# Turns for VectorE's two-operand work and GpSimd's work in the plan of an attention, expert layer and gated experts kernel

## The chip, the cores and the metric

The program runs on one core of a Trainium2 chip. The core has five engines that run side by side, each through its own queue of instructions in a fixed order, and that wait for each other through semaphores: TensorE (PE: matrix products; PEld is its loading of weights), VectorE (DVE), ScalarE (ACT), GpSimd (POOL) and SyncE (SP), which here only issues transfers. TensorE writes its results to PSUM; the working data of all engines lie in SBUF. The metric is the time of one execution on the device in microseconds (us); 1 ns is a thousandth of that.

## The reference

Three layers follow each other, all in float32; 4 x 576 = 2304 tokens, 512 wide.

```python
# band attention: 8 heads of 64, each query sees itself and the 127 before it
scores = scale * np.matmul(q, k.transpose(0, 1, 3, 2))
scores = np.where(mask, scores + bias[None], -1000000000.0)
attn = np.exp(scores - np.max(scores, axis=-1, keepdims=True))
attn = attn / (np.sum(attn, axis=-1, keepdims=True) + 1e-09)
x = np.matmul(attn, v)                     # then heads side by side: 2304 x 512
# first layer, 512 -> 2048 -> 512
h = np.maximum(x @ w_in, 0.0)
x = h * h @ w_out
# eight experts, 512 -> 1024 -> 512, weighted by a gate
P = np.exp(x @ w_gate - (x @ w_gate).max())
for _ in range(8):
    P /= P.sum(1, keepdims=True) + 1e-09
    P /= P.sum(0, keepdims=True) + 1e-09
    P *= N / E
for e in range(E):
    out += P[:, e:e + 1] * (np.maximum(x @ w1[e], 0.0) @ w2[e])
```

## The kernel before

**Numbers as pairs.** Each operand of a large product is split into a float16 part and a float16 remainder ("hi" and "lo"), and three of the four partial products are added. So each tile that feeds TensorE is made in two steps: ScalarE rounds it to hi (`g_hi`, `h_hi`, `ex_hi`, `t_hi`, ...), and then VectorE or GpSimd subtracts hi from the original and writes lo (`g_lo`, `ex_lo`, `t_lo` on VectorE; `h_lo`, `e_lo`, `w_lo` through the helper `minus` on GpSimd). Such a subtraction reads two operands from SBUF.

**The experts.** They take the last 1400 us or so. The eight experts of 1024 hidden columns are worked off in 16 groups `g` of 512 (half an expert), each for five blocks `j` of tokens (four blocks of 512 tokens and one, `j` = 1, of 256), in two parts `p`. Each block product is done as a 2 x 2 product with seven multiplications in place of eight, which costs sums of weights and of results. For a part the functions are:

- `g_prod` (L1427, TensorE): the seven products x @ w1, into the banks X, Y and Z of PSUM, six matrix products each of 256 columns (128 for the narrow block). `g_copy` (L1455, ScalarE) copies a bank to SBUF; `g_add` (L1459, VectorE) adds a bank of PSUM to such a copy ("a" from Z, "b" from Y, "c" from X); `g_relu` (L1467, ScalarE).
- `g_sum` (L1476 and, through `minus`, L396, GpSimd): four sums of the results, S1, S3, S2, S4, one after the other, each with two operands from SBUF. `g_hi` (L1486, ScalarE) and `g_lo` (L1490, VectorE) make the seven pairs `hp` for the second product.
- `o_prod` (L1509, TensorE): the seven products with w2, into banks oX, oY, oZ. `o_add` (L1535, VectorE) adds a bank, times the gate, to the output sums `acc_wc`, `acc_wd` and `x1`; two instructions in a wide block.
- the weights of a later group, while this one runs: `ex_load` (SyncE), `ex_sumsq` and `ex_scale` (a scale from the sum of squares), `ex_hi` (L1325, ScalarE) and `ex_lo` (L1329, VectorE) of the weights themselves, `ex_sums` (L1339 and L396 on `stage`, GpSimd: four sums), then `ex_hi` and `ex_lo` of these sums, 1024 columns in one instruction. `gates` (L1644, VectorE) makes the gate of the group.

**What sets the order.** The whole kernel is first written as some 11,000 units with an engine, a cost, a rank, the units that they wait for, and the buffers that they take and free (`unit` and `chain`, the class `Plan`). `Plan.run` then plays the program through with these costs: whenever an engine is free, it takes, of the units that are ready and whose buffers are free, the one with the lowest rank. The order in which units were taken is the order in which their instructions are written, engine by engine. On the chip only that order and the semaphores remain. Most units of the experts have the same lowest rank (`GEMM`) on VectorE, ScalarE and GpSimd, so the one that became ready first is taken; weight steps have a higher rank and come when nothing else is ready. The costs say, for 256 columns, 0.34 us on VectorE and 0.61 (0.69 for a `g_sum`) on GpSimd:

```python
    def c_dve(n, rate=1.04):
        return 0.07 + n * rate * 1e-3

    def c_pool(n):
        return 0.12 + n * 1.93e-3
```

## Time and profile before

| | |
|---|---|
| median of 3 runs | 2012.65 us (2009.2 to 2021.81) |
| the profiled execution, its own time | 2018.5 us |
| its span, first to last instruction | 2016.6 us |
| busy: TensorE | 1919.4 us (95%) |
| busy: VectorE | 1625.6 us (81%) |
| busy: ScalarE | 1259.6 us (62%) |
| busy: GpSimd | 982.9 us (49%) |
| TensorE's granted clock, mean | 0.99 of full |

The busy share of an engine is a mean over stages that differ, and ends of matrix products are modelled. A wait is told as engine, line and what released it. Lines are those of the kernel before; in the kernel after, lines behind the changed places stand 11 further on (L1490 is L1501, L1459 is L1470, L1535 is L1546, L1329 is L1340).

### The profile page before, as it was taken

What the parts mean: (1) busy time and instruction counts of PE and PEld (TensorE: products, weight loads), DVE (VectorE), ACT (ScalarE), POOL (GpSimd) and SP (SyncE); (2) the same over time, 40 slices, a digit from 0 to 9 for tenths busy, and PEclk for the clock granted to TensorE, in tenths of its full rate; (3) what the DMA queues carried; (4) which work ended last, traced back from release to release, by engine and by line L of the source; (5) the groups of instructions that cost most, each with busy time, mean ns of one, the idle gap of its engine ahead of it and who ended that gap; (6) DMA issues with size and microseconds to landing.
All of it is one profiled execution on the core that took longest, in us unless ns stands there. A gap on an engine that the chain in (4) does not pass through costs nothing.

```text
span 2016.6 us, 47090 instructions
## 1 busy us (share of the span) xinstructions
PE 1919.4 (95%) x18458; PEld 1689.7 (84%) x18458; DVE 1625.6 (81%) x3897; ACT 1259.6 (62%) x3434; POOL 982.9 (49%) x1198
## 2 busy tenths in 40 slices
PE   9799999999998899999999999999999999999999
PEld 9677888787886788888888888888888888888888
DVE  7797576464339988998989989898998989899887
ACT  6667576453346776766666666666666666666654
POOL 3444254357527554454545455454554545545432
PEclk9899999999999999999999999999999999999999
DMA  9343364220010010000101001000100101010002
GB/s 241 94 147 75 72 120 78 38 64 1 1 43 12 32 33 19 25 25 20 43 12 33 22 22 37 18 33 12 33 22 23 43 12 33 12 33 12 1 22 74
DMA packets 159662, 85.35 MB, mean 42 GB/s; under 512 B 112080, under 2 KB 144848, under 8 KB 159440
## 3 DMA queue, kind: packets, MB, share of 16 engines
q1 hardware_dynamic: 159440, 82.35, 15.7%
q8 instruction: 144, 2.36, 0.5%
q14 instruction: 78, 0.64, 0.1%
HBM read 64.50 MB, written 4.72 MB: 34 GB/s over the span
## 4 chain that ended last, share of the span: by engine, by line
PE 44%; DVE 33%; POOL 7%; ACT 6%; issue 6%; DMA 3%; SPq 0%; POOLq 0%; DVEq 0%; ACTq 0%
DVE hp L1490 10%; PE X L1427 9%; PE oX L1509 7%; PE h L1021 6%; PE y L1058 6%; DVE late L1329 6%; PE Y L1427 4%; PE oY L1509 3%; DMA stage<-in_moe_w_dram 2%; DVE acc_wc L1535 2%; DVE acc_wd L1535 2%; POOL stage L396 2%; DVE late L1459 2%; PE Z L1427 2%; ACT late L1325 2%
## 5 line engine op out<-in xcount | busy, mean ns | idle before, releaser
L1427 PEld LDWEIGHTS <-late 128*128 128x128 f16 x6720 | 617.7, 98 | 135.3 <-issue 67.8
L1509 PEld LDWEIGHTS <-hp 128*128 128x128 f16 x6048 | 585.8, 98 | 74.8 <-issue 9.9
L1509 PE MATMUL oX<-late,hp 128*128 128x256 f16 x3456 | 467.8, 273 | 5.9 <-DVE acc_wd L1535 4.1
L1490 DVE TENSOR_TENSOR hp<-late,hp 128x256 f16<-128x256 f32 (+1 forms) x662 | 317.8, 498 | 23.7 <-ACT hp L1486 19.7
L1486 ACT ACTIVATE hp<-late 128x256 f16<-128x256 f32 (+1 forms) x662 | 245.5, 388 | 72.4 <-POOL late L396 63.9
L1490 DVE TENSOR_TENSOR hp<-x,hp 128x256 f16<-128x256 f32 (+1 forms) x458 | 239.2, 531 | 25.6 <-ACT hp L1486 20.0
L1427 PE MATMUL Y<-y,late 128*128 128x256 f16 (+1 forms) x1920 | 241.3, 262 | 7.6 <-ACT late L1455 2.5
L1427 PE MATMUL X<-late 128*128 128x256 f16 (+1 forms) x1728 | 204.8, 254 | 35.3 <-DVE x L1459 16.8
L1509 PE MATMUL oY<-late,hp 128*128 128x256 f16 x1728 | 237.2, 273 | 0.0
L1021 PE MATMUL h<-xT,w_in 128*128 128x256 f16 x1728 | 221.0, 277 | 8.0 <-ACT r L1030 6.5
L1058 PE MATMUL y<-sq,w_out 128*128 128x256 f16 x1728 | 218.0, 274 | 0.9 <-DVE y L1126 0.9
L396 POOL TENSOR_TENSOR sq<-r,sq 128x256 f16<-128x256 f32 x144 | 108.5, 755 | 216.0 <-ACT sq L1044 210.2
L396 POOL TENSOR_TENSOR stage<-stage 128x256 f32<-128x256 f32 x210 | 178.9, 852 | 67.6 <-DVE late L1329 57.1
L1486 ACT ACTIVATE hp<-x 128x256 f16<-128x256 f32 (+1 forms) x458 | 174.1, 389 | 37.1 <-POOL x L396 27.3
L1467 ACT ACTIVATE late<-late 128x256 f32<-128x256 f32 (+1 forms) x295 | 114.8, 392 | 130.9 <-DVE late L1459 130.3
L1021 PEld LDWEIGHTS <-w_in 128*128 128x128 f16 x1728 | 169.1, 100 | 31.9 <-issue 8.6
L1058 PEld LDWEIGHTS <-w_out 128*128 128x128 f16 x1728 | 166.4, 99 | 23.8 <-issue 1.3
L396 POOL TENSOR_TENSOR late<-late 128x256 f32<-128x256 f32 (+1 forms) x211 | 170.0, 807 | 27.5 <-DVE hp L1490 15.3
L1329 DVE SCALAR_TENSOR_TENSOR late<-stage,es,late 128x512 f16<-128x512 f32 (+1 forms) x180 | 173.3, 988 | 4.5 <-ACT late L1325 2.9
L1325 ACT ACTIVATE late<-stage,es 128x512 f16<-128x512 f32 (+1 forms) x180 | 135.1, 783 | 43.0 <-POOL stage L396 37.4
L1427 PE MATMUL X<-form,late 128*128 128x256 f16 x1152 | 157.8, 273 | 3.4 <-DVE late L1459 2.6
L1036 DVE SCALAR_TENSOR_TENSOR r<-r,unit_s 128x256 f32<-128x256 f32 x112 | 68.5, 613 | 108.8 <-ACT r L1030 108.2
(230 smaller groups left out, 3093.1 us busy)
## 6 DMA issues: line engine op xcount, KB each, us to landing
stage<-in_moe_w_dram SPq DMA_DIRECT2D x60, 256.0 KB, 3.2
stage<-in_moe_w_dram SPq DMA_DIRECT2D x30, 512.0 KB, 3.7
st_in<-in_moe_w_in_dram SPq DMA_DIRECT2D x16, 512.0 KB, 6.5
st_out<-in_moe_w_out_dram SPq DMA_DIRECT2D x16, 512.0 KB, 5.5
raw_q<-in_q_dram SPq DMA_DIRECT2D x16, 256.0 KB, 4.7
raw_k<-in_k_dram SPq DMA_DIRECT2D x16, 256.0 KB, 4.5
raw_v<-in_v_dram SPq DMA_DIRECT2D x16, 256.0 KB, 4.5
out_dram<-acc_wc SPq DMA_DIRECT2D x8, 256.0 KB, 2.9
```

Of the source, the lines that this page charges most:

```text
L396: POOL.tensor_tensor(out=dst, in0=src, in1=hi, op=ALU.subtract)
L1021: PE.matmul(hp, lhsT=w[:, a, kk, r], rhs=xT[parts1[m][0]][:, b, kk, c : c + MC], start=(kk == 0 and a == b), stop=(kk == KD - 1 and a == LO),)
L1036: DVE.scalar_tensor_tensor(out=r, in0=r, scalar=unit_s[:, 1, g : g + 1], in1=r, op0=ALU.mult, op1=ALU.mult)
L1058: PE.matmul(hold["y", d // 2][:, d % 2], lhsT=w[:, a, f % FPC, d * P : (d + 1) * P], rhs=sq[:, b], start=(first and d % 2 == 0 and a == b) ...
L1325: ACT.activation(out=hi, in_=t, func=ACTF.Copy, scale=es[:, g, 2 * kind + 1 : 2 * kind + 2])
L1329: DVE.scalar_tensor_tensor(out=lo, in0=t, scalar=es[:, g, 2 * kind + 1 : 2 * kind + 2], in1=hi, op0=ALU.mult, op1=ALU.subtract)
L1427: PE.matmul(pt, lhsT=w[:, a, row(kk), :], rhs=rhs, start=(x in (1, 2, 5) and kk == 0 and a == c), stop=(x in (2, 3, 4) and kk == KH - 1 an ...
L1467: ACT.activation(out=t, in_=src, func=ACTF.Relu)
L1486: ACT.activation(out=f[:, HI], in_=hold["t", PLACE[name], g, j, p], func=ACTF.Copy)
L1490: DVE.tensor_tensor(out=f[:, LO], in0=hold["t", PLACE[name], g, j, p], in1=f[:, HI], op=ALU.subtract)
L1509: PE.matmul(pt[:, t], lhsT=f[:, a, t * P : (t + 1) * P], rhs=w[:, c, row], start=(x in (1, 2, 5) and p == t == 0 and a == c), stop=(x in ( ...
L1535: DVE.scalar_tensor_tensor(out=A[:, t], in0=pt[:, t], scalar=pd[:, g, i + t : i + t + 1], in1=A[:, t], op0=ALU.mult, op1=ALU.add)
```

## The change

A unit gets a mark, `shared`. It is set for every unit of GpSimd and for the VectorE units of ten functions, most of which read two operands from SBUF (`PORT`). `Plan.run` keeps one holder and the time until which it holds: a marked unit isn't taken while the other engine's marked unit runs in the plan. Units that aren't marked are taken meanwhile, whatever their rank. When a hold ends, VectorE is asked before GpSimd, since its units come first in the program. The costs, ranks and buffers are the same, and so are the instructions; each engine has the same number of them.

```diff
--- before.py
+++ after.py
@@ -21,9 +21,11 @@
         self.engine, self.cost, self.emit, self.rank, self.lag, self.until = engine, cost, emit, rank, lag, until
         self.name = ""
         self.waits, self.then, self.takes, self.nth, self.frees = 0, [], [], [], []
+        self.shared = False
 
 
 class Plan:
+
 
 
 
@@ -78,6 +80,7 @@
             if not u.waits:
                 ready[u.engine].append(u)
         now, left = 0.0, len(self.units)
+        held, until = None, 0.0
         while left:
             moved = True
             while moved:
@@ -85,11 +88,15 @@
                 for eng, units in ready.items():
                     if free_at[eng] > now:
                         continue
-                    fit = [u for u in units if fits(u)]
+                    fit = [
+                        u for u in units if fits(u) and not (u.shared and held is not eng and until > now + 1e-6)
+                    ]
                     if not fit:
                         continue
                     u = min(fit, key=lambda x: x.rank)
                     units.remove(u)
+                    if u.shared:
+                        held, until = eng, now + u.cost
                     if u.until is not None and now > u.until:
                         u.cost, u.emit = 0.0, lambda: None
                     for t in u.takes:
@@ -323,11 +330,14 @@
     plan.lags.update({PE: 0.2, ACT: 0.22, DVE: 0.22, POOL: 0.22})
     plan.own_lag.update({PE: 0.0, ACT: 0.06, DVE: 0.06, POOL: 0.06})
     GEMM, LATER = -1000000, 1000000
+
+    PORT = {"g_lo", "ex_lo", "t_lo", "v_lo", "x_lo", "x_hi", "narrow", "join_v", "prep_gate", "h_square"}
     WARM, COLD, IDLE = 230, 24, 66.0
 
     def unit(engine, cost, f, *args, **kw):
         u = plan.add(engine, cost, lambda: f(*args), **kw)
         u.name = (f.__name__, args)
+        u.shared = engine is POOL or f.__name__ in PORT
         return u
 
     def chain(engine, costs, f, *args, rank, after=(), take=(), lag=None):
@@ -342,6 +352,7 @@
         for c in costs:
             u = plan.add(engine, c, step, rank=rank, after=after, take=take, lag=lag)
             u.name = (f.__name__, args)
+            u.shared = engine is POOL or f.__name__ in PORT
             after, take = [u], ()
             us.append(u)
         return us
```

What this does to the order, at three places of the steady part, where the last block of group 4 is followed by the first of group 5. Ahead is VectorE's queue around the sum of bank Z of group 5, block 0, part 0 (L1459, `Z5_0_0`). L1490 on `hp` is `g_lo`, L1535 `o_add`, L1329 the weights' `ex_lo`. Before:

```order
L1490 TENSOR_TENSOR hp0_8325<-late_6170,hp0_8325 128x256
L1535 SCALAR_TENSOR_TENSOR acc_wd_8621<-oY4_3_14597,pd_92,acc_wd_8621 128x256 x2
L1329 SCALAR_TENSOR_TENSOR late_6170<-stage_8208,es_87,late_6170 128x1024
L1490 TENSOR_TENSOR hp0_8325<-late_6170,hp0_8325 128x256
L1490 TENSOR_TENSOR hp0_8325<-x1_8297,hp0_8325 128x256
L1459 TENSOR_TENSOR late_6170<-Z5_0_0_14645,late_6170 128x256
L1490 TENSOR_TENSOR hp1_8326<-late_6170,hp1_8326 128x256
L1535 SCALAR_TENSOR_TENSOR acc_wd_8621<-oX4_3_14474,pd_92,acc_wd_8621 128x256 x2
```

After (L1501 is `g_lo`, L1470 `g_add`, L1546 `o_add`, L1340 `ex_lo`):

```order
L1501 TENSOR_TENSOR hp0_8325<-late_6184,hp0_8325 128x256
L1501 TENSOR_TENSOR hp1_8326<-x1_8297,hp1_8326 128x256
L1470 TENSOR_TENSOR late_6184<-Z5_0_0_14640,late_6184 128x256
L1546 SCALAR_TENSOR_TENSOR acc_wd_8600<-oX4_3_14474,pd_92,acc_wd_8600 128x256 x2
L1501 TENSOR_TENSOR hp1_8326<-late_6184,hp1_8326 128x256 x2
L1340 SCALAR_TENSOR_TENSOR late_6184<-stage_8208,es_87,late_6184 128x1024
L1501 TENSOR_TENSOR hp0_8325<-x1_8297,hp0_8325 128x256
L1546 SCALAR_TENSOR_TENSOR acc_wd_8600<-oY4_3_14594,pd_92,acc_wd_8600 128x256 x2
```

The sum of Z has moved from behind the 1024-column weight piece and two `g_lo` to a place ahead of that piece, and a second `g_lo` and a pair of `g_lo` stand ahead of the piece too.

The second place is VectorE's queue some 20 instructions on, around the sums of banks Y and X of part 1 (`Y5_0_1`, `X5_0_1`). L1306, L231, L236, L239 and L1643 are the small steps of the next group's weight scale and gate, L1644 is `gates`. Before:

```order
L1490 TENSOR_TENSOR hp0_8325<-x1_8297,hp0_8325 128x256
L1490 TENSOR_TENSOR hp1_8326<-late_6170,hp1_8326 128x256
L1459 TENSOR_TENSOR late_6170<-Z5_0_1_14781,late_6170 128x256
L1490 TENSOR_TENSOR hp1_8326<-x1_8297,hp1_8326 128x256
L1490 TENSOR_TENSOR hp0_8325<-late_6170,hp0_8325 128x256
L1329 SCALAR_TENSOR_TENSOR late_6170<-stage_8208,es_87,late_6170 128x512
L1329 SCALAR_TENSOR_TENSOR late_6170<-stage_8208,es_87,late_6170 128x256
L1490 TENSOR_TENSOR hp0_8325<-x1_8297,hp0_8325 128x256
L1490 TENSOR_TENSOR hp0_8325<-late_6170,hp0_8325 128x256
L1535 SCALAR_TENSOR_TENSOR acc_wd_8621<-oZ4_4_14802,pd_92,acc_wd_8621 128x256 x2
L1459 TENSOR_TENSOR late_6170<-Y5_0_1_14792,late_6170 128x256
L1459 TENSOR_TENSOR x1_8297<-X5_0_1_14759,x1_8297 128x256
```

After (L1317, L238, L243, L246, L1654 are the small steps, L1655 is `gates`):

```order
L1501 TENSOR_TENSOR hp0_8325<-late_6184,hp0_8325 128x256 x2
L1317 TENSOR_REDUCE emg_14827<-total_14799 128x1
L1546 SCALAR_TENSOR_TENSOR acc_wd_8600<-oZ4_4_14789,pd_92,acc_wd_8600 128x256 x2
L1470 TENSOR_TENSOR late_6184<-Y5_0_1_14778,late_6184 128x256
L238 TENSOR_SCALAR pn1_14846<-emg_14827 128x1
L243 TENSOR_SCALAR es_87<-pn1_14846 128x1
L1501 TENSOR_TENSOR hp1_8326<-late_6184,hp1_8326 128x256
L246 RECIPROCAL es_87<-es_87 128x1
L1654 TENSOR_TENSOR gs_14858<-es_87 128x1
L1655 SCALAR_TENSOR_TENSOR pd_92<-prob_91,gs_14858,typ_89 128x18
L1470 TENSOR_TENSOR late_6184<-X5_0_1_14739,late_6184 128x256
L1546 SCALAR_TENSOR_TENSOR acc_wd_8600<-oX4_4_14729,pd_92,acc_wd_8600 128x256 x2
```

The weight piece of 512 and 256 columns that stood ahead of both sums now comes behind them; the small steps and `gates`, which came seven rows ahead of this piece before, now stand between the two sums.

The third place is GpSimd's queue at the same turn of groups. `stage` are the weights of `ex_sums`, `late` and `x1` the results of `g_sum`. Before:

```order
L396 TENSOR_TENSOR x1_8297<-x1_8297,late_6170 128x256
L1339 TENSOR_TENSOR stage_8208<-stage_8208 128x2x128
L396 TENSOR_TENSOR stage_8208<-stage_8208 128x2x128 x3
L1476 TENSOR_TENSOR x1_8297<-x1_8297 128x256
L396 TENSOR_TENSOR x1_8297<-x1_8297,late_6170 128x256
L396 TENSOR_TENSOR late_6170<-x1_8297,late_6170 128x256
L396 TENSOR_TENSOR late_6170<-late_6170 128x256
L1476 TENSOR_TENSOR late_6170<-late_6170,x1_8297 128x256
```

After (L1350 and L407 on `stage` are `ex_sums`, L1487 and L407 on the others `g_sum`):

```order
L407 TENSOR_TENSOR late_6184<-late_6184,x1_8297 128x256
L1350 TENSOR_TENSOR stage_8208<-stage_8208 128x2x128
L407 TENSOR_TENSOR stage_8208<-stage_8208 128x2x128 x2
L1487 TENSOR_TENSOR x1_8297<-x1_8297,late_6184 128x256
L407 TENSOR_TENSOR stage_8208<-stage_8208 128x2x128
L407 TENSOR_TENSOR late_6184<-late_6184,x1_8297 128x256
L407 TENSOR_TENSOR x1_8297<-x1_8297 128x256
L407 TENSOR_TENSOR late_6184<-late_6184,x1_8297 128x256
```

The four weight sums stood in a row; now the first sum of the running part (L1487) comes ahead of the fourth.

## Rows read from the trace of the kernel before

**Rows 1.** Busy time by stage: columns are engines, instructions in brackets, clock, DMA.
```profile
0.00:610.00 610.00, 572.35 (x5696) 496.20 (x5697) 371.17 (x967) 341.45 (x879) 279.94 (x313) 0.98 0.35 81
610.00:700.00 90.00, 76.33 (x684) 65.50 (x684) 83.05 (x208) 61.02 (x165) 54.38 (x62) 0.94 0.07 24
700.00:1900.00 1200.00, 1159.20 (x11024) 1028.10 (x11023) 1078.33 (x2502) 797.51 (x2221) 610.13 (x772) 1.00 0.08 24
```

**Rows 2.** Longest pieces of the chain of waits, whole span: start us, us, what.
```profile
43.57 2.19 DVE st_out L884
...
950.56 2.05 issue
...
1823.39 2.05 issue
```

**Rows 3.** Chain of waits in 1008:1035 by line, a piece; then 1035:1062.
```profile
by line: PE X L1427 33.6%; PE oX L1509 28.3%; PE Y L1427 14.6%; PE oY L1509 12.1%; PE Z L1427 7.3%; PE oZ L1509 4.9%
...
1032.05 1.31 PE oX L1509 x12
...
by line: DVE hp L1490 24.8%; issue 13.4%; DVE acc_wd L1535 10.5%; ACT late L1325 8.4%; POOL stage L396 8.2%; DVE late L1329 7.3%; POOL stage L1339 4.4%; ACT hp L1486 3.8%; DVE late L1459 3.7%; PE X L1427 3.0%; POOL x L396 2.7%; DVE x L1459 
```

**Rows 4.** TensorE's waits in 700:1900: us in total, times, longest.
```profile
PE X L1427 <- DVE late L1459: 12.2, 19, 1.1
PE X L1427 <- DVE x L1459: 11.2, 21, 0.8
...
PE oX L1509 <- ACT acc_wd L1530: 0.2, 1, 0.2
```

**Rows 5.** Groups by shape, 700:1900: busy us, mean ns, idle before, releaser.
```profile
L1490 DVE TENSOR_TENSOR hp<-late,hp 128x256 f16<-128x256 f32 x456 | 226.2, 512 | 19.4 <-ACT hp L1486 15.8
...
L1490 DVE TENSOR_TENSOR hp<-x,hp 128x256 f16<-128x256 f32 x312 | 176.2, 572 | 20.4 <-ACT hp L1486 15.3
...
L1329 DVE SCALAR_TENSOR_TENSOR late<-stage,es,late 128x1024 f16<-128x1024 f32 x55 | 87.1, 1583 | 3.9 <-ACT late L1325 2.4
...
L1459 DVE TENSOR_TENSOR late<-Z,late 128x256 f32<-128x256 f32 x107 | 44.3, 414 | 7.8 <-ACT late L1455 4.8 <-ACT hp L1486 2.0 <-PE Z L1427 0.7
...
L1644 DVE SCALAR_TENSOR_TENSOR pd<-prob,gs,typ 128x18 f32<-128x18 f32 x14 | 10.5, 752 | 0.5
```

**Rows 6.** Timeline, a free and a caught pair: start, us, engine, instruction [idle].
```profile
1029.20 0.74 DVE L1490 TENSOR_TENSOR hp<-late,hp 128x256 f16<-128x256 f32 x2
...
1036.80 0.73 POOL L396 TENSOR_TENSOR x<-x,late 128x256 f32<-128x256 f32 x1 [0.42 <-DVE hp L1490]
...
1036.91 1.23 DVE L1490 TENSOR_TENSOR hp<-x,hp 128x256 f16<-128x256 f32 x2
```

**Rows 7.** Timeline of 1044 to 1053 us, VectorE and TensorE.
```profile
1044.33 0.82 PE L1427 MATMUL Z<-y,late 128*128 128x256 f16 x6
...
1044.45 1.76 DVE L1329 SCALAR_TENSOR_TENSOR late<-stage,es,late 128x1024 f16<-128x1024 f32 x1
...
1047.33 0.41 DVE L1459 TENSOR_TENSOR late<-Z,late 128x256 f32<-128x256 f32 x1
...
1052.82 0.82 PE L1427 MATMUL X<-y,late 128*128 128x256 f16 x6
```

**Rows 8.** Timeline of 1053 to 1062 us, VectorE and TensorE.
```profile
1053.08 0.15 DVE L1306 TENSOR_REDUCE emg<-total 128x1 f32<-128x2 f32 x1
...
1058.80 0.94 DVE L1490 TENSOR_TENSOR hp<-late,hp 128x256 f16<-128x256 f32 x1
...
1059.66 0.86 DVE L1535 SCALAR_TENSOR_TENSOR acc_wd<-oZ,pd,acc_wd 128x256 f32<-128x256 f32 x2
...
1060.78 0.41 DVE L1459 TENSOR_TENSOR x<-X,x 128x256 f32<-128x256 f32 x1
...
1061.24 0.81 PE L1427 MATMUL X<-late 128*128 128x256 f16 x6 [0.40 <-DVE x L1459]
```

**Rows 9.** TensorE's longest named wait in 0:610.
```profile
PE s L582 <- DVE nmax L596: 12.0, 14, 2.7
```

## The prediction

> **What bounds the kernel now.** I read the stage table first [rows 1]. From 700 us on nothing changes any more but the index of the weight group: TensorE is busy in 1159 of 1200 us at full clock, VectorE in 1078, GpSimd in 610. Ahead of it lie 610 us of attention and the first expert layer, and 90 us of changeover. The long pieces of the chain of waits give the period of the steady part: a piece of 2.05 us comes back at 950.56 and, ten groups on, at 1823.39 [rows 2], so a group takes 87.3 us.
>
> TensorE needs less. Six products of 256 columns take 0.655 us where nothing stops them (twelve in 1.31, [rows 3]). By the code a group has 714 such products (two parts, four wide blocks of 84 each, and 42 of the narrow block) and 84 of 128 columns; the trace agrees (11024 in 1200 us are 802 in 87.3). 714 / 6 x 0.655 is 77.9, and the 84 narrow ones at half that price, an estimate, 4.6, together 82.5 us. So 4.8 us of each group are lost, 77 us over the 16 groups.
>
> Where they go: in one third of a group (1008 to 1035) the chain is all TensorE; in the next (1035 to 1062) it is mostly VectorE, L1490 in front with 24.8%, and TensorE has 3% or so [rows 3]. TensorE's named waits in the steady part come to 38.1 us in eleven rows, and the first two, for L1459 (`g_add`), are 23.4 of them, 61% [rows 4]. `g_add` itself is never slow: 414 ns as a mean against 0.41 in single pieces [rows 5, 8]. It is late because of what stands ahead of it in VectorE's queue. That is `g_lo` (L1490), which has two operands in SBUF: the same 256 columns, but a mean of 512 and 572 ns [rows 5]. The timeline shows why. A pair of them takes 0.74 us alone; the pair that begins 0.11 us after a GpSimd operation takes 1.23 [rows 6]. So the two engines take turns, and VectorE's queue stands still during GpSimd's turn. Over 414 ns the 456 and 312 wide ones lose 45 and 49 us in 1200, 6.8 us in a group, and the weight pieces (L1329, mean 1583 for 1024 columns) some more. The old plan knows nothing of it.
>
> **The change part by part.** No instruction is added or removed. What an engine executes stays as it is; the order in which the plan hands it out changes, on VectorE, GpSimd, ScalarE and, less, on TensorE and SyncE's loads. Three parts of it have a price.
>
> First, the steady part. Where the plan believes that GpSimd is at its turn, VectorE is now given what needs no turn: `g_add` and `o_add`, which read PSUM. The first order piece shows it: the sum of the Z bank is moved from behind the 1024-column weight piece and two `g_lo` to a place ahead of that piece. In the trace that sum began at 1047.33, although the product that it reads began at 1044.33 and took 0.82: the piece (1.76 us) and two `g_lo` stood in between [rows 7]. The second piece shows the sums of Y and X. In the trace a `g_lo` blocked for 0.94 us at 1058.80 stands ahead of them, the X sum begins at 1060.78, and TensorE's next product waits for it until 1061.24 [rows 8].
>
> The ceiling is all 4.8 us in a group, the floor nothing. The waits for GpSimd do not vanish: GpSimd and the two-operand work have the same lengths as before, and the plan will let VectorE stand at the port where nothing else is ready. What goes is the wait of a sum behind them. I therefore take the share of TensorE's waits that names `g_add`, 61% of 4.8, 2.9 us. Against it stands what the second piece also shows: four of the five tiny scale steps and `gates` (L1644), which reads two operands in SBUF but is not on the list, now come between the Y and the X sum, once in a group. A tiny step takes 0.15 us [rows 8], L1644 0.75 as a mean for 18 columns, so it too is caught by GpSimd [rows 5], and a `g_lo` of 0.41 goes along: if the X sum is due just then this costs up to 4 x 0.15 + 0.75 + 0.41 = 1.8 us, if it is not yet due nothing; I take 0.5. That leaves 2.4 us in a group, 38 us in 16.
>
> Second, GpSimd. The third order piece shows that its four weight sums no longer run in a row; one sum of the running pair comes between them. With the four moved back, the weights of the next part are complete later. In the trace the 1024-column piece ends at 1046.20, and the first product of its part begins at 1052.82: 6.6 us to spare [rows 7]. On VectorE the piece now stands behind one more `g_lo` and the Z sum (0.41 each), one more `o_add` pair (0.86, [rows 8]) and a pair of `g_lo` (0.74 to 1.23, [rows 6]): 2.4 to 2.9 us. GpSimd's part is one more operation of 0.73 [rows 6]. At most 3.6 of 6.6 us are used up: nothing is lost, as long as that cover holds.
>
> Third, the first 700 us. There TensorE is idle in the records for 38 us of 610 and 14 of 90 [rows 1], and the longest of its named waits is 12 us for the bias step (L596) [rows 9]. The new order puts some of the long weight steps behind bias steps. That may win those 12 us; but weight steps of 2.19 us [rows 2] that come later may hold up the first layer, and five of them in a row would cost 11. I take 0, with 10 either way. The changeover (VectorE busy in 83 of 90 us) is taken at 0, at best 5.
>
> The sum is 38 us. The profiled execution took 2018.5 us (2016.6 of span); 2018.5 - 38 is 1980.5. The median of the runs is 2012.65, and 38 off that is 1975 us.
>
> **A rule weighed.** In the row, the pair caught by GpSimd takes 0.49 us more than a free one, while GpSimd's operation had 0.62 us to go [rows 6], so VectorE gets in before GpSimd's recorded end. The Trainium skill ("SBUF — State Buffer", "A bandwidth-pool intuition that's wrong (but worth ruling out)") has the loser blocked until the other's end plus about 115 ns. By it each caught pair would have lost 0.74 and each turn would cost more than the plan charges; the row shows less, and the sum goes by the row.
>
> **The rivals.** (a) The waits only move. The plan's turns hold on the chip only if the two engines arrive as planned; a GpSimd operation that is ready a few tenths early takes the port, and VectorE, whose two-operand work now stands directly behind GpSimd's, waits as long as before. For it: the 6.8 us of waiting in a group belong to work that stays; a plan whose steps are 0.34 us long is upset by little. Against it: the waits that matter are those with a `g_add` behind them, and their number falls by order, not by timing. It gives back 0 to 0.8 us a group: 2000 to 2013, say 2005.
> (b) The weights come late, and the kernel gets slower. Place: the 1024-column pieces and GpSimd's sums, moved back as above. It decides when a part's weights are moved by more than 6.6 us against its first product. Then that product, and in TensorE's fixed queue all behind it, waits each group. At 3 us a group that is 48 us; with half of the 38 kept, 2012.65 + 29 is 2041. For it: GpSimd's weight sums (L1339, and L396 on `stage`) and ScalarE's L1325 hold 21% of the chain from 1035 to 1062 [rows 3], so this work is not loose. Against: I count 3.6 of 6.6.
> (c) The port is the bound. GpSimd's 772 operations at 0.73 are at most 564 us of 1200, the 768 wide `g_lo` at 0.41 at most 315, the 55 long pieces 87: 966 us, 80%, while TensorE needs 82.5 / 87.3, 94%. To decide, each turn would have to cost 0.2 us more than the rows show, and then it would hold before as well. Time 2012; I give it no chance of its own but count it with (a).
> The rule above would add 115 ns to each of 772 turns, 89 us: by that estimate 1055 of 1200, 88%, still under TensorE's need, so it changes no chance.
>
> **How the numbers follow.** A change under 1%, 20 us, is about what a measurement of this kernel can't tell from none. Forecast (gain 1 to 4.8 us a group): 0.68. Rival (a), with the case that the gain is under 1%: 0.21. Rival (b), or a first layer that loses over 30 us: 0.11. Low end: 4 us a group (64) and 5 from the start, 1944. High end: the lower edge of (a) and 5 us lost at the start, 2018. Outside are half of (b) with 0.11 and a gain over 68 us with about 0.06. Faster by over 1% (under 1992.5): 0.68; within 1%: 0.22; slower: 0.10.
>
> **What would show it.** Right: the period falls from 87.3 to about 85; TensorE's waits for the sums fall from 23.4 us in 1200 to under 12; the share of the chain that lies on L1490 falls; `g_lo` still shows means above 414 ns, since GpSimd's work is the same. The 610 us ahead stay within 10. Wrong: the same period with the same `g_lo` means and the same waits is (a); a first product of a part that waits for L1340 (L1329 now) is (b); a gain or loss that lies ahead of 610 us is neither, and then the third part was mis-sized.

## The result, and the profile after

The kernel after takes 1940.42 us (median of 4 runs, 1939.28 to 1941.46), the kernel before on the same chip 2011.93 (4 runs): a ratio of 0.9635, interval 0.9614 to 0.9657. The direction of the forecast was right, its size was not. It gave a gain of 38 us; the gain is 71.5, and the time lies below the low end of the range (1944).

The chain that ended last by engine, from the page of the kernel before; then busy time of each engine and the same chain from the page of the kernel after.

```profile
PE 44%; DVE 33%; POOL 7%; ACT 6%; issue 6%; DMA 3%; SPq 0%; POOLq 0%; DVEq 0%; ACTq 0%
```

```profile
PE 1893.8 (98%) x18458; PEld 1680.8 (87%) x18458; DVE 1605.7 (83%) x3897; ACT 1256.2 (65%) x3434; POOL 938.6 (48%) x1198
...
PE 82%; DVE 11%; ACT 3%; DMA 2%; issue 1%; POOL 0%; SPq 0%; DVEq 0%; POOLq 0%; ACTq 0%
```

The chain is now 82% TensorE, where it was 44%; GpSimd has left it. Its span is 1939.5 us, 77.1 less than that of the profile before (that execution was itself 6.6 us over the median of the runs). The 77.1 us are read from marks that both programs have, the first expert product of each group: group 0 begins at 591.6 before and at 559.1 after, which is **32.5 us**; the 14 groups from 1 to 14 take 87.3 us each before and 84.2 after, **43.0** (unrounded) in all; group 0 gives 1.0, and all behind the last mark 0.6.

The steady part first. The stage table of the kernel after, beside [rows 1]:

```profile
0.00:610.00 610.00, 587.03 (x5948) 511.79 (x5949) 390.98 (x1053) 358.67 (x938) 285.88 (x330) 0.99 0.36 82
610.00:700.00 90.00, 83.77 (x790) 72.89 (x788) 82.33 (x186) 65.81 (x176) 56.33 (x67) 1.00 0.06 19
700.00:1900.00 1200.00, 1188.30 (x11410) 1065.29 (x11408) 1105.00 (x2595) 817.69 (x2285) 587.23 (x789) 1.00 0.08 26
```

In 1200 us TensorE does 11410 products where it did 11024, 3.5% more. Its idle time there falls from 40.8 us to 11.7. The rest shows as fewer busy nanoseconds for a product, 1188.30 / 11410 = 104.1 in place of 105.2. That too comes from the pauses: a six (six products of 256 columns) is recorded at 0.82 us [rows 7], but where another follows it counts 0.655 [rows 3], since its end overlaps the next one's start; the full 0.82 count only ahead of a pause.

TensorE's named waits of the kernel after in 700:1900 (us in total, times, longest), beside [rows 4]:

```profile
PE X L1438 <- DVE x L1470: 5.2, 7, 1.4
PE X L1438 <- DVE late L1470: 4.6, 7, 0.8
```

23.4 us of waiting for `g_add` are now 9.8. But VectorE's groups by shape in 700:1900 (busy us, mean ns, idle before), beside [rows 5], do not show why:

```profile
L1501 DVE TENSOR_TENSOR hp<-late,hp 128x256 f16<-128x256 f32 x482 | 261.8, 561 | 6.7 <-ACT hp L1497 4.9
L1501 DVE TENSOR_TENSOR hp<-x,hp 128x256 f16<-128x256 f32 x323 | 185.5, 583 | 10.2 <-ACT hp L1497 9.0
...
L1340 DVE SCALAR_TENSOR_TENSOR late<-stage,es,late 128x1024 f16<-128x1024 f32 x56 | 76.6, 1368 | 0.4 <-ACT late L1336 0.4
...
L1655 DVE SCALAR_TENSOR_TENSOR pd<-prob,gs,typ 128x18 f32<-128x18 f32 x13 | 3.2, 246 | 0.5
```

The weight pieces and `gates` (246 ns for 752) are caught by GpSimd less often, but the mean `g_lo` has become *longer*: 561 and 583 ns for 512 and 572. Over all two-operand instructions of VectorE the time beyond their free length is 11.8 us a group after and 10.9 before (groups 2 to 13; for each shape, the sum over its fastest tenth). So on the chip VectorE was held up as much as before. GpSimd was held up less: one of its operations takes 587.23 us / 789 = 744 ns as a mean, where it took 610.13 / 772 = 790 [rows 1]. That may be a part of the gain; the run with mean lengths below has most of the steady gain without it (599.00 us / 755 = 793 ns in 700:1850).

One collision recurs in every group. It stands in the chain of waits of the kernel after, whole span (start us, us, what), one group apart:

```profile
961.55 1.70 DVE hp L1501 x2
1045.59 1.70 DVE hp L1501 x2
...
1801.99 1.70 DVE hp L1501 x2
```

From 961.55 to 1801.99 are ten groups, 84.04 us each. The timeline of the kernel after, VectorE, GpSimd and then TensorE, at the second one (start, us):

```profile
1045.18 0.41 DVE L1470 TENSOR_TENSOR late<-Y,late 128x256 f32<-128x256 f32 x1
1045.51 1.78 DVE L1501 TENSOR_TENSOR hp<-x,hp 128x256 f16<-128x256 f32 x2
1047.21 0.41 DVE L1470 TENSOR_TENSOR late<-X,late 128x256 f32<-128x256 f32 x1
...
1045.41 0.73 POOL L407 TENSOR_TENSOR stage<-stage 128x256 f32<-128x256 f32 x1
1046.09 0.91 POOL L407 TENSOR_TENSOR x<-x,late 128x256 f32<-128x256 f32 x1
...
1047.67 0.81 PE L1438 MATMUL X<-late 128*128 128x256 f16 x6 [0.66 <-DVE late L1470]
```

Two `g_lo` take 1.78 us where a free pair takes 0.74 [rows 6], the sum of X stands behind them, and TensorE stands still for 0.66 us. In 970:1055 it is TensorE's only named wait.

Now the first 591.6 us, cut at the products of the first layer with the same number. Columns as in [rows 1]; the clock is the last but two. Before:

```profile
48.00:136.00 88.00, 73.95 (x663) 62.60 (x661) 69.14 (x162) 56.63 (x134) 40.12 (x35) 0.90 0.46 128
136.00:230.00 94.00, 88.46 (x782) 75.05 (x780) 66.45 (x189) 65.99 (x172) 38.95 (x39) 0.96 0.42 93
230.00:401.00 171.00, 165.53 (x1755) 140.82 (x1753) 104.04 (x306) 100.89 (x289) 72.76 (x83) 1.00 0.38 72
401.00:501.00 100.00, 93.08 (x931) 81.32 (x930) 55.27 (x112) 43.75 (x100) 63.13 (x71) 0.98 0.15 35
501.00:591.00 90.00, 90.00 (x851) 80.79 (x850) 29.74 (x63) 30.91 (x75) 37.70 (x46) 1.00 0.05 14
```

After:

```profile
49.00:127.00 78.00, 74.00 (x714) 64.67 (x712) 65.63 (x175) 62.09 (x151) 39.90 (x36) 0.98 0.49 122
127.00:207.00 80.00, 77.56 (x705) 65.42 (x705) 55.86 (x170) 59.14 (x154) 37.19 (x38) 1.00 0.54 124
207.00:376.00 169.00, 166.44 (x1768) 142.14 (x1767) 103.09 (x308) 101.95 (x292) 71.47 (x82) 1.00 0.39 71
376.00:468.00 92.00, 90.74 (x930) 80.12 (x928) 51.60 (x107) 42.46 (x96) 48.87 (x58) 1.00 0.16 39
468.00:559.00 91.00, 90.47 (x854) 80.96 (x852) 37.43 (x68) 32.11 (x79) 48.92 (x58) 1.00 0.06 16
```

The gain sits in three stretches. The first two take 182 us before and 158 after. TensorE idles 19.6 us of them before and 6.4 after, 13.2 less; the granted clock costs 88 x 0.10 + 94 x 0.04 = 12.6 us before and 78 x 0.02 = 1.6 after, 11.0 less. That is 24.2 of the 24. The fourth stretch is 8 us shorter: 5.6 less idle, 2.0 less from the clock. So some 13 of 32.5 us came through TensorE's clock, which fell to its lower level (1.2 GHz) around pauses; an idle stretch at that level counts in both sums, so this is an estimate. One such place, in VectorE's and then TensorE's timeline of the kernel before:

```profile
63.27 2.08 DVE L880 SCALAR_TENSOR_TENSOR bits_out<-st_out,bits_out 128x1024 int32<-128x1024 int32 x1
65.27 0.89 DVE L1038 TENSOR_TENSOR r<-r 128x256 f32<-128x256 f32 x1
66.08 2.19 DVE L884 SCALAR_TENSOR_TENSOR st_out<-st_out,bits_out 128x1024 int32<-128x1024 int32 x1
68.31 1.04 DVE L876 TENSOR_SCALAR bits_out<-st_out 128x1024 int32<-128x1024 int32 x1
69.39 2.07 DVE L880 SCALAR_TENSOR_TENSOR bits_out<-st_out,bits_out 128x1024 int32<-128x1024 int32 x1
71.48 1.95 DVE L884 SCALAR_TENSOR_TENSOR st_out<-st_out,bits_out 128x1024 int32<-128x1024 int32 x1
73.36 0.47 DVE L596 CUSTOM_DVE_ANT_0 e<-s,bands,slope 128x256 f32<-128x256 f32 x1
...
74.30 0.80 PE L582 MATMUL s<-kT,qT 64*128 64x128 f32 x4 [2.70 <-DVE nmax L596]
```

The window ahead of it and the one behind it, same kernel and columns as above:

```profile
62.00:72.00 10.00, 9.04 (x122) 8.09 (x119) 9.86 (x11) 6.60 (x17) 10.00 (x7) 1.00 0.18 30
73.00:83.00 10.00, 8.70 (x43) 7.50 (x43) 2.76 (x15) 5.52 (x17) 0.00 (x0) 0.50 0.01 2
```

`narrow` (L876, L880, L884) makes 32-bit numbers of the first layer's weights, which come as two words each, 1024 columns a step. Each two-operand step here is caught by GpSimd, which is busy in all 10 us from 62 to 72: 2 us, against 1.22 where one is free (below). The bias step (L596) comes after all of them, the scores wait for it 2.70 us, and for the next 10 us the clock is 0.50. In the kernel after, VectorE's timeline at the same work alternates:

```profile
66.60 1.55 DVE L891 SCALAR_TENSOR_TENSOR bits_out<-st_out,bits_out 128x1024 int32<-128x1024 int32 x1
...
68.51 0.35 DVE L607 CUSTOM_DVE_ANT_0 e<-s,bands,slope 128x128 f32<-128x128 f32 x1 [0.26 <-PE s L593]
...
69.05 1.22 DVE L895 SCALAR_TENSOR_TENSOR st_out<-st_out,bits_out 128x1024 int32<-128x1024 int32 x1
70.36 0.35 DVE L607 CUSTOM_DVE_ANT_0 e<-s,bands,slope 128x128 f32<-128x128 f32 x1
```

TensorE's waits for the bias step, in the two stretches up to 230 and 207 us, before and then after:

```profile
PE s L582 <- DVE nmax L596: 9.6, 9, 2.7
```

```profile
PE s L593 <- DVE nmax L607: 1.0, 1, 1.0
```

### The profile page after: what moved, and what is told of

Same layout as the page of the kernel before. It is cut to its first block, busy times and chain, and to the rows that moved or that the text cites. A ratio compares the mean times of both kernels' runs of the same rounds, so it can differ in the third digit from the quotient of the medians.

```text
span 1939.5 us, 47163 instructions
## 1 busy us (share of the span) xinstructions
PE 1893.8 (98%) x18458; PEld 1680.8 (87%) x18458; DVE 1605.7 (83%) x3897; ACT 1256.2 (65%) x3434; POOL 938.6 (48%) x1198
## 4 chain that ended last, share of the span: by engine, by line
PE 82%; DVE 11%; ACT 3%; DMA 2%; issue 1%; POOL 0%; SPq 0%; DVEq 0%; POOLq 0%; ACTq 0%
PE oX L1520 17%; PE X L1438 16%; PE h L1032 9%; PE oY L1520 8%; PE y L1069 8%; PE Y L1438 8%; PE Z L1438 4%; PE oZ L1520 4%; DVE hp L1501 4%; PE s L593 2%; DVE late L1340 1%; DMA stage<-in_moe_w_dram 1%; PE av L654 1%; PE warm L291 1%; PE t L569 1%
## 5 line engine op out<-in xcount | busy, mean ns | idle before, releaser
L1501 DVE TENSOR_TENSOR hp<-late,hp 128x256 f16<-128x256 f32 (+1 forms) x669 | 337.4, 524 | 10.1 <-ACT hp L1497 8.1
L1501 DVE TENSOR_TENSOR hp<-x,hp 128x256 f16<-128x256 f32 (+1 forms) x451 | 242.9, 549 | 14.7 <-ACT hp L1497 13.3
L1032 PE MATMUL h<-xT,w_in 128*128 128x256 f16 x1728 | 216.4, 274 | 0.0
L407 POOL TENSOR_TENSOR sq<-r,sq 128x256 f16<-128x256 f32 x144 | 106.7, 742 | 211.4 <-ACT sq L1055 204.3
L1069 PEld LDWEIGHTS <-w_out 128*128 128x128 f16 x1728 | 166.4, 98 | 23.5 <-issue 1.7
L407 POOL TENSOR_TENSOR stage<-stage 128x256 f32<-128x256 f32 x210 | 168.5, 803 | 34.4 <-ACT hp L1497 21.9
L1340 DVE SCALAR_TENSOR_TENSOR late<-stage,es,late 128x512 f16<-128x512 f32 (+2 forms) x180 | 158.5, 909 | 0.7 <-ACT late L1336 0.6
L1047 DVE SCALAR_TENSOR_TENSOR r<-r,unit_s 128x256 f32<-128x256 f32 x112 | 68.7, 616 | 100.7 <-ACT r L1041 99.9
L1478 ACT ACTIVATE x<-x 128x256 f32<-128x256 f32 (+1 forms) x194 | 74.5, 389 | 118.0 <-DVE x L1470 117.3
L1487 POOL TENSOR_TENSOR late<-late 128x256 f32<-128x256 f32 (+1 forms) x58 | 45.7, 787 | 196.1 <-DVE hp L1501 170.1
```

Of the source, the lines that this page charges most:

```text
L407: POOL.tensor_tensor(out=dst, in0=src, in1=hi, op=ALU.subtract)
L1032: PE.matmul(hp, lhsT=w[:, a, kk, r], rhs=xT[parts1[m][0]][:, b, kk, c : c + MC], start=(kk == 0 and a == b), stop=(kk == KD - 1 and a == LO),)
L1047: DVE.scalar_tensor_tensor(out=r, in0=r, scalar=unit_s[:, 1, g : g + 1], in1=r, op0=ALU.mult, op1=ALU.mult)
L1069: PE.matmul(hold["y", d // 2][:, d % 2], lhsT=w[:, a, f % FPC, d * P : (d + 1) * P], rhs=sq[:, b], start=(first and d % 2 == 0 and a == b) ...
L1340: DVE.scalar_tensor_tensor(out=lo, in0=t, scalar=es[:, g, 2 * kind + 1 : 2 * kind + 2], in1=hi, op0=ALU.mult, op1=ALU.subtract)
L1478: ACT.activation(out=t, in_=src, func=ACTF.Relu)
```

## The experiments

Three questions: which marks make which part of the gain; whether it takes turns, or only a plan with truer lengths; and whether the steady gain is room in TensorE's queue (more of other products ahead of the one that reads a sum). "Period" is the mean length of the groups 2 to 13, "start" the first expert product of group 0, both of the profiled execution; before 87.35 and 591.6, after 84.20 and 559.1. "Waits" are TensorE's waits for `g_add` in 700:1850: before 21.8 us, after 9.8. All twelve were timed against the kernel before on the same chip (medians 2016.05, 2015.0 and 2013.95).

### Which marks

**Marks only on the units of routing and experts**, made in the last call:

```diff
+    turns = [False]
-        u.shared = engine is POOL or f.__name__ in PORT
+        u.shared = turns[0] and (engine is POOL or f.__name__ in PORT)
...
+        turns[0] = True
         plan_experts(closed, opened, *plan_routing(closed))
```

> Only the units of the last stage (routing forms, experts and their weights) are marked; attention and the first layer are planned as before. Against 2011.9 before and 1940.4 after. If the gain has two independent parts (45 us in the experts, 32 us ahead of the first product with w1, as the two traces split it), the first product with w1 begins near 590 us as before, the period of a group is near 84 us, and the time is 1962 to 1972. If the early gain is a by-product of the experts' marks, it is 1940 to 1948.

1970.54 us, 0.9771 (0.9744 to 0.9798). Period 84.30, start 592.1: the whole steady gain. The start seems to be the old one, but two things cancel in it. Every engine's order is that of the kernel before up to 436 us, and yet this execution came to the cut at 401 only at 407.1 (granted clock in 40:240 0.91, before 0.94). From there, the stretch that took 99.9 us before and 92.1 after (fourth row of the tables above, between products of the first layer with the same number) took 93.0. In the same window, kernel before and then this run:

```profile
400.00:600.00 200.00, 191.50 (x1854) 169.19 (x1853) 88.22 (x187) 80.92 (x189) 100.83 (x116) 0.99 0.11 29
```

```profile
400.00:600.00 200.00, 196.02 (x1905) 172.98 (x1904) 86.46 (x189) 82.58 (x193) 101.29 (x119) 1.00 0.11 29
```

So the experts' marks make 5 to 7 us ahead of the experts too (the run with room alone, whose order there is that of the kernel before, took 97.7).

**Marks only on attention and first layer**: the same edit with `True` and `False` exchanged.

> Only attention and the first layer are marked; routing and experts are planned as before. If the parts are independent, the first product with w1 begins near 560 us, the period stays at 87.2 us, and the time is 1975 to 1985. If the experts' marks made the early gain, it is 2005 to 2015.

1991.04 us, 0.9875 (0.9853 to 0.9897), between the two expectations. Period 87.25, start 568.1. The two gains, 45.5 and 25.0 us, add up to 70.5 of 71.5: they are two effects. This one makes 23.5 of the 32.5 us at the start. The other 9 are the fourth stretch, 101.1 us here, where the weights of the experts are already worked on: it takes 92.1 to 93.2 us in every run with marks on the experts, be there marks on the first part or not.

**The same without `narrow`**, by which I tried the early mechanism:

```diff
-    PORT = {"g_lo", "ex_lo", "t_lo", "v_lo", "x_lo", "x_hi", "narrow", "join_v", "prep_gate", "h_square"}
+    PORT = {"v_lo", "x_lo", "x_hi", "join_v", "prep_gate", "h_square"}
```

> As e2_first, but the weight steps of narrow (L887 to L895, 1024 columns of int32) are taken off the list; GpSimd and the other functions keep their turns in the first part. If the early gain comes from narrow giving way to the bias steps, most of it is gone: the first product with w1 begins at 580 us or later and the time is 2000 to 2012. If it comes from the other turns, it is 1975 to 1988 as in e2_first.

2001.92 us, 0.9933 (0.9911 to 0.9955), as expected of the first branch. Its start, 584.2, is that of the slowest of its five executions (2008.8), so the medians are the better measure: of the 25.0 us of the run before, `narrow`'s turns make 10.9.

**No turns, but `narrow` planned at 1.35 times its cost**, about its mean on the chip:

```diff
-                        DVE, c_dve(n, 0.52 if y == 0 else 1.04), narrow, kind, g, x, y, rank=z + 1,
+                        DVE, 1.35 * c_dve(n, 0.52 if y == 0 else 1.04), narrow, kind, g, x, y, rank=z + 1,
```

> No marks; narrow alone costs 1.35 times as much in the plan, as its mean in the trace before was against its free length. If the early gain comes from planning these steps at their real length, the first product with w1 begins at 570 to 580 us and the time is 1995 to 2005; if it needs the turns themselves (bias ahead of a narrow that would meet GpSimd), it begins at 587 us or later and the time is 2008 to 2020.

1998.11 us, 0.9913 (0.9889 to 0.9937), start 575.9: 15.7 us at the start and 16.9 in the medians, without a turn. Here it is the length that the plan gives `narrow` that acts. But it does not act through the bias step alone. TensorE's waits of this kernel in 40:240:

```profile
PE s L593 <- DVE nmax L607: 8.7, 6, 2.5
```

Its windows at the same place:

```profile
40.00:240.00 200.00, 188.14 (x1754) 162.48 (x1752) 151.21 (x397) 139.56 (x350) 91.04 (x86) 0.97 0.43 112
```

It still waits 8.7 us for that step. In the same window the kernel before idles 19.6 us at a clock of 0.94, this one 11.9 at 0.97, the kernel after 6.5 at 0.99. The start follows all of TensorE's pauses, and the clock that goes with them.

### Turns or lengths

**No turns, but the plan's costs raised to the means of the trace** (GpSimd by 1.2, `g_lo` and `t_lo` by 1.4, the others of the list by 1.15):

```diff
+    def longer(engine, f):
+        if engine is POOL:
+            return 1.2
+        if f.__name__ in ("g_lo", "t_lo"):
+            return 1.4
+        return 1.15 if f.__name__ in PORT else 1.0
...
+        cost *= longer(engine, f)
-        u.shared = engine is POOL or f.__name__ in PORT
+        u.shared = False
```

> No marks. The plan is told mean lengths instead: GpSimd's units cost 1.2 times, g_lo and t_lo 1.4 times, the other listed functions 1.15 times as much, roughly what the waits made of them in the trace before. If it is the turns (what may stand ahead of what) that win, this wins little: 1990 to 2012, a period of 86 us or more. If it is enough that the plan leaves more room behind this work, it wins most of the 72 us: 1940 to 1965.

1954.77 us, 0.9694 (0.9676 to 0.9711): period 84.79, start 571.4, waits 12.9. Without any turns 2.56 of 3.15 us in a group come, and 20.2 of 32.5 at the start.

**VectorE's lengths alone** (the same without GpSimd's 1.2).

> As e3_means (no marks, mean lengths), but only VectorE's listed functions are longer in the plan; GpSimd costs what it did. If what the plan lacked is VectorE's time at the port, this keeps most of e3's steady gain: a period of 84.6 to 85.3 us and 1955 to 1975. If GpSimd's later results were the point, the period is 86.5 us or more and the time 1990 to 2015.

1980.12 us, 0.9824 (0.9802 to 0.9845), period 86.04, between the two expectations; waits 12.1, but waits for `g_copy`, on ScalarE, come in their place (10.4 us).

**GpSimd's lengths alone** (1.2 on `g_sum` and `ex_sums`, nothing else).

> No marks; only g_sum and ex_sums of GpSimd cost 1.2 times as much in the plan. If VectorE's time at the port is what the plan lacked, the period stays above 86.5 us and the time is 2000 to 2020. If GpSimd's later results were the point, the period is near 85 us and the time 1965 to 1985.

1999.1 us, 0.9914 (0.9883 to 0.9945), period 86.16, waits 25.1; again between the two expectations. The one gives 1.3 us in a group and the other 1.2; together 2.5, what the run with both gave (2.56). So the length of either engine counts, about equally, and neither is the whole.

### Room for the sums

**No turns; the plan takes the result of `g_add` as there 0.72 us after its end** (0.22 before), so that TensorE's queue has other products ahead of the one that reads it:

```diff
-        u.shared = engine is POOL or f.__name__ in PORT
+        u.shared = False
...
-            return unit(DVE, c_dve(n), g_add, g, j, p, x, rank=GEMM, after=after)
+            return unit(DVE, c_dve(n), g_add, g, j, p, x, rank=GEMM, after=after, lag=0.72)
```

> No marks, costs as before, but the plan believes that the result of g_add reaches the other engines 0.5 us later (a lag of 0.72 instead of 0.22 us). TensorE's queue then has 3.9 products from the seventh to the fourth product of a part, where it had 3.3 before and has 3.8 with the turns; VectorE and GpSimd take no turns in the plan. If the steady gain of the turns is this room in TensorE's queue, the period falls from 87.3 to 84 to 85 us and the time is 1965 to 1980. If it is the order on VectorE (sums ahead of two-operand work), the period stays above 86.5 and the time is 2000 to 2015.

2024.43 us, 1.0049 (1.0028 to 1.0069): period 88.01, waits 31.2. It is slower than the kernel before, which neither expectation had. TensorE's waits of this kernel in 700:1850:

```profile
PE X L1438 <- DVE late L1470: 16.3, 33, 0.7
PE X L1438 <- DVE x L1470: 14.9, 25, 0.8
```

Room alone gave nothing where the plan has wrong lengths: the rest of the order moved too, and TensorE waited longer for the sums.

**Turns, but less room** (`g_add` planned at 0.1 us, its result there at once; this also hides its own 0.41 us from the plan):

```diff
-            return unit(DVE, c_dve(n), g_add, g, j, p, x, rank=GEMM, after=after)
+            return unit(DVE, 0.1, g_add, g, j, p, x, rank=GEMM, after=after, lag=0.0)
```

> The marks of the change are kept, but the plan believes that g_add costs 0.1 us and that its result is there at once, so the fourth product stands only 2.4 products behind the seventh (3.8 in the changed kernel). If room in TensorE's queue makes the steady gain, the period is back at 87 us or more and the time is 1985 to 2030; the early gain stays. If the order on VectorE makes it, the period stays under 85 us and the time is 1940 to 1955.

1974.96 us, 0.9803 (0.978 to 0.9826): period 86.36, start 559.1, waits 13.7, between the two expectations. Of 3.15 us in a group 2.16 are gone, and products wait for `g_copy` (L1466) as well. TensorE's waits in 700:1850:

```profile
PE Y L1438 <- ACT late L1466: 11.5, 10, 1.3
PE X L1438 <- DVE late L1470: 9.5, 25, 1.0
PE X L1438 <- DVE x L1470: 4.2, 14, 0.8
```

**Turns and more room** (the kernel after with a lag of 0.72).

> The changed kernel, and g_add's result 0.5 us later in the plan (4.2 products from the seventh to the fourth). If TensorE's remaining waits for the sums, 9.8 us in 1150 of the steady part, go as well, the period falls from 84.2 to about 83.3 and the time is 1922 to 1935; if what remains has another cause it is 1936 to 1945.

1935.5 us, 0.9605 (0.9581 to 0.9628): period 83.65, waits 0.5. The start, 566.2, is 7.1 later than after's: TensorE's clock fell at 142 us in this profile.

**Turns, with GpSimd's operations planned 0.04 us longer** (256 columns at 0.65 us instead of 0.61; the trace has 0.73 [rows 6]):

```diff
-        return 0.12 + n * 1.93e-3
+        return 0.16 + n * 1.93e-3
```

> The changed kernel with GpSimd's cost in the plan 0.04 us higher for each operation (0.73 for a g_sum of 256 columns, as in the trace, instead of 0.69). If the rest of the steady loss (84.2 against 82.5 us) comes from turns that the plan ends too early, the period falls below 84 us and the time is 1925 to 1938; if not, it is 1937 to 1950.

1956.89 us, 0.9713 (0.9687 to 0.9739), slower than the kernel after, which neither expectation had: period 84.93, waits 17.9, and yet `g_lo` is caught less: its mean, of both kinds of 256 columns, is 525 ns in groups 2 to 13 (before 534, after 569), and VectorE's time beyond free lengths is 10.2 us a group (after 11.8). **Fewer collisions, but more waiting of TensorE, and a truer length that made the kernel slower.** It also shows how far a small change of one cost moves the whole order: 0.04 us in the plan, 0.73 us in a group.

**The same and a lag of 0.52 us for `g_add`**:

```diff
-            return unit(DVE, c_dve(n), g_add, g, j, p, x, rank=GEMM, after=after)
+            return unit(DVE, c_dve(n), g_add, g, j, p, x, rank=GEMM, after=after, lag=0.52)
```

> As e11_turns_true, and g_add's result 0.3 us later in the plan. If room for the sums adds to true turns as it added to the turns in e8_turns_room, the period is 83.2 to 83.7 us and the time 1920 to 1932; if the two do the same, it is as e11_turns_true.

1933.58 us, 0.9595 (0.9573 to 0.9617), the fastest of all: period 83.48, one us over the 82.5 that the products alone need. TensorE's waits of this kernel in 700:1850:

```profile
PE X L1438 <- DVE late L1470: 2.3, 5, 1.0
...
PE X L1438 <- DVE x L1470: 0.6, 2, 0.3
```

Its larger group of `g_lo` in 700:1900, by shape:

```profile
L1501 DVE TENSOR_TENSOR hp<-late,hp 128x256 f16<-128x256 f32 x485 | 232.5, 498 | 8.0 <-ACT hp L1497 7.0
```

Against the kernel after the difference is small (0.9595 beside 0.9635; their intervals touch), but the period and the waits say the same. The two kernels with turns and more room are also the ones whose `g_lo` is caught least, 501 ns here and 514 in the run with a lag of 0.72 (groups 2 to 13), so fewer collisions may be a part of their gain; the run before this one shows that these alone do not make it.

## Why the prediction failed, step by step

**The step that failed is the third part, the first 700 us.** It took 0, with 10 either way, and the place gave 32.5 (some 27 in the medians: 71.5 less the 44.6 below). The prediction saw the 12 us for the bias step and set against them that "weight steps of 2.19 us [rows 2] that come later may hold up the first layer, and five of them in a row would cost 11". Five steps of `narrow`, with one other instruction among them, stood in the kernel *before*, at 63 to 73 us, and the change took them apart. So it set 12 against 11, and the row of five was no loss to come: it stood there already. Three terms were left out. One is the rest of TensorE's idle time: 19.6 us of it up to 230 us and 6.9 from 401 to 501, of which the bias step is a part. The second is the clock: the 0.98 of [rows 1] was in the prediction's own first row, and 610 x 0.02 is 12 us, about the 13 that the clock gave back. The third is that the experts' marks act ahead of the experts, from 436 us on (5 to 7 us). With idle time and clock in the sum the bound for that part would have been some 50 us (38 idle, 12 clock), not 12.

**What is shown of this part**: what the plan holds of `narrow` is the cause of 11 us (its turns) to 17 us (its length by a factor, without turns), and the experts' marks are the cause of 5 to 9 us in the fourth stretch. **What stays open**: the rest of the early gain, and which unit of the experts' weights decides the fourth stretch. With the marks on the first part alone TensorE's clock fell near 408 and 449 us, at pauses of 1.34 and 2.75 us; in the kernel after those pauses are absent. A start read from one execution is good to some 6 us only: one and the same order came to the cut at 401 us at 401.5 in the kernel before and at 407.1 in the run with marks on the experts, and the clock differed.

**First term, steady part**: the place and the direction were right, the size was low: 3.15 us in a group (2.4 forecast), 44.6 us of span with group 0 and the end (38 forecast). The share of 61% was low: 4.8 us were lost in a group, 2.9 taken ahead of the charge, and 3.87 us are there to be had, as the best kernel shows (87.35 to 83.48). The other waits, for `o_add` and `g_copy`, fell along with those for `g_add`. The charge of 0.5 for `gates` did not come up: the step is now free of GpSimd, 0.25 us. Another, of nearly the same size, stands in its place (0.66 us at 1047.67). Without the charge the forecast, 2.9, would have been close to the 3.15; with that stop counted in the place of the charge, the share should have given 3.8 of the 4.8.

**Its reason was half right.** It was that a sum no longer stands behind a blocked `g_lo`. The waits for `g_add` fell as said (23.4 to 9.8), but not through the turns as such: mean lengths in place of turns give 2.56 of 3.15 us. My reading, argued and not shown, is that turns and mean lengths do the same: they tell the plan how long the work of both engines takes where they meet, and the plan then orders everything else, ScalarE's copies and TensorE's products among it, by times that are nearer to the chip's. Against it stands the run with GpSimd's longer cost: nearer to the trace, and 0.73 us a group slower until the sums had more room. On room: without lengths 88.01; with turns 84.20, and 83.65 with more; with turns and the longer cost 84.93, and 83.48 with more. So room helped only where the lengths were in the plan. That taking it away costs 2.16 us is less clear, since that run also made `g_add` too short. How much of it is a `g_add` that comes earlier and how much a product that comes later is not separated. Nor was a rival tried: any change of the costs gives another order, and no run changed them by as much the wrong way. All four runs with longer costs and no turns were faster than the kernel before, which speaks against mere chance but does not exclude it.

**Second term, GpSimd's weight sums**: nothing, as forecast. No wait of TensorE in the steady part names L1340; the cover of 6.6 us held.

**The rivals.** (a) had its premise right: VectorE waits as long at the port as before, and the mean `g_lo` grew. Its conclusion was wrong: the length of these waits does not set the time by itself, and the run with the longer GpSimd costs (less of this waiting, 16 us slower than the kernel after) says so a second time. (b) did not come. (c) fell with (a): at 84.2 us a group the engines still had the same instructions to run.

**The rule weighed** (the Trainium skill, "SBUF — State Buffer", "A bandwidth-pool intuition that's wrong (but worth ruling out)") has the loser blocked to the other's end plus some 115 ns; that section of the Trainium skill measured it on a transfer whose descriptors GpSimd cannot write until VectorE lets go of the port, and here it is VectorE that waits. In the kernel after, the caught pair at 1045.51 lasts 1.78, 1.04 more than a free one, over two GpSimd operations. These begin at 1045.41 (0.73 us) and 1046.09 (0.91), so the pair ends at 1047.29, 0.29 behind the recorded end of the second one. A free `g_lo` takes 0.37 (half of a free pair), so the second `g_lo` was let in ahead of that end. By the rule it would have ended near 1047.5, an estimate.

## What to carry to other kernels

Where a plan orders the instructions, look first at the instructions whose length on the chip differs most from the plan's, and give the plan that length; a rule that makes two engines take turns is one way to do so, a factor another, and both act far from the place of the collision. Time each step of it: one truer length made this kernel 16 us slower until the sums had more room. Then give the result that TensorE waits for some tenths of a us more room: here room helped only after the lengths were right. A clock mean below 1.00 in a stage is a sum to be written down (1 minus the mean, times the stage), since a change that removes pauses can give it back too, as 13 us here.

## What the runs showed of the hardware that was not expected

In the kernel before TensorE's clock fell where the engine paused: with the wait of 2.70 us shown above the granted clock was 0.50 from 73 to 83 us, and it fell again at 93 behind a pause of 2.95 and at 476 behind one of 1.76. Four products of the scores took 0.80 us there and 0.50 at full clock (60.32 us, kernel before). So a pause cost more than its own length: ten us at half clock are five us of full clock's work. One order, run again, took 5.6 us more for its first 401 us, at a granted clock of 0.91 in 40:240 for 0.94. And an 18-column operation with two operands in SBUF (`gates`) took 787 to 797 ns in 13 of its 14 steady executions, in each with a GpSimd operation of 0.73 us that began 0.03 us behind its start; the one that met none took 244, and the mean of the kernel after is 246. So a short instruction lost as much there, 0.54 us, as a caught `g_lo` in the kernel after (0.95 at 1043.91 for 0.41 free).
